# Gated sum of two state-space layers: loading the second stage's weights early, splitting SBUF between the stages, and folding C inside the first token block

## The chip, the cores and the metric

The kernel runs on one core of one Trainium2 chip, as a single launch. The metric is the device time in microseconds (us). Before the change its median over 6 runs is 695.59 us (694.76 to 696.88).

The core's engines each work through a list of instructions of their own, in order: TensorE (PE, matmul), VectorE (DVE, elementwise), ScalarE (ACT, activations and scaled copies), GpSimd (POOL) and SyncE (SP), which here only issues DMA transfers. "SPq" and "ACTq" in a profile are the queues in which SP and ACT issue them. The lists are written by a scheduler, which also decides the order within an engine; a tile pool decides when a piece of SBUF becomes free for its next user.

## The reference

One input `x` of 2048 tokens x 1024 channels goes through two layers, whose outputs are mixed by a gate per token:

```python
    x = A_x
    g = _sigmoid((x * gate_w).sum(-1, keepdims=True))
    a = _A_ref(x, A_Lambda_re, A_Lambda_im, A_B_re, A_B_im, A_C_re, A_C_im, A_log_dt, A_Dskip)
    b = _B_ref(x, B_k, B_v, B_shift_k, B_ssm_k, B_ssm_D)
    return g * a + (1 - g) * b
```

Layer A is a diagonal complex recurrence over the tokens, with a dense complex matrix before and after it:

```python
        B_bar = ((Lam_bar - 1.0) / Lam)[:, None] * Bmat
        Bu = jnp.einsum("bld,pd->blp", x + 0j, B_bar)
        ...                      # for each token t:  h = Lam_bar * h + Bu[t]
        y = 2.0 * jnp.einsum("blp,dp->bld", hseq, Cmat).real + x * Dskip[None, None, :]
```

Layer B is a short convolution of `k`, a product with `v`, a long causal convolution over all 2048 tokens (by FFT), and a product with `q`, which is `x` here:

```python
        kv = k_shift * v
        ...                      # y = irfft(rfft(kv) * rfft(ssm_k)), causal, per channel
        y = y + kv * ssm_D[None, None, :]
        return q * y
```

## The kernel before

It has two stages. Stage B does layer B in the frequency domain, in two channel halves (`dh`) of 512 channels and, in each, four time blocks of 512 tokens. The `P` operations are on DVE and the rest is matmuls with cosine and sine tables:

```python
        for dh in range(NDH):                       # NDH = 2
            ...   # kpc: 4 tiles of ssm_k by transposing DMA (two buffers); kT, vT by transposing DMA
            ...   # acc = short convolution x v (ACT tmpj, DVE acc), PE transposes it into kvT
            ...   # Kre, Kim = spectra of kpc (PE, copied out by ACT)
            for b in range(4):
                ...   # Vre, Vim = spectra of kvT (PE, copied out by ACT)
                for s in range(b, 4):
                    ...   # Pre, Pim += K x V (complex): 6 DVE operations for b = 0, else 8
                s = b
                xblkB = bxb.tile([128, NBT, DHW], BF16, name="xblkB")
                nc.sync.dma_start(out=xblkB, in_=xf[s * B:(s + 1) * B, d0:d0 + DHW]...)
                pbB = bblk.tile([128, NBT, DHW], BF16, name="pbB")
                for tl in range(NBT):               # NBT = 4
                    ...   # psc = inverse transform of P (8 or 16 matmuls)
                    cv = bblk.tile([128, DHW], BF16, name="cv")
                    nc.scalar.activation(out=cv, in_=psc, func=ACT.Copy)
                    nc.vector.tensor_tensor(out=pbB[:, tl, :], in0=cv, in1=xblkB[:, tl, :], op=ALU.mult)
                nc.sync.dma_start(out=pB_scr[...], in_=pbB)      # parked in HBM for stage A
```

Stage A opens its own pools when those of stage B have closed. It first loads and prepares weights:

```python
        nc.scalar.dma_start(out=gwb, ...)           # gate weights
        nc.scalar.dma_start(out=dsk, ...)           # Dskip
        ...   # BTre, BTim: 16 transposing DMAs of 128 x 1024, on SP
        xT_next = load_xT_block(0)                  # 8 transposing DMAs of 128 x 512, on SP
        for pi in range(NP):                        # NP = 8: rotation tables TBs, TBc
            ...   # DVE: ht, rqtab, frtab   ACT: fatab (Abs), TBs (Sin), TBc (Sin)
        for pi in range(NP):                        # folding C with the input scale
            nc.sync.dma_start_transpose(out=cre, in_=A_C_re[:, pi * 128:(pi + 1) * 128])
            nc.sync.dma_start_transpose(out=cim, in_=A_C_im[:, pi * 128:(pi + 1) * 128])
            nc.scalar.activation(out=t1, in_=cre, func=ACT.Identity, scale=col(c2r, pi))
            ...   # t2, t3, t4 alike: 4 ACT operations of 128 x 1024
            nc.vector.tensor_tensor(out=cre, in0=t1, in1=t2, op=ALU.add)
            nc.vector.tensor_tensor(out=cim, in0=t3, in1=t4, op=ALU.add)
```

Then it goes over four blocks (`tb`) of 512 tokens:

```python
            for pi in range(NP):
                ...   # bu_re, bu_im: 8 matmuls each (PE); bure, buim: copies (ACT)
                ...   # DVE: rotate (6 operations), two scans Wre and Wim, rotate back into hb_re, hb_im (6)
            for tl in range(TT_B):                  # TT_B = 4 tiles of 128 tokens
                ...   # pbb: load of pB_scr
                for dh in range(NDH):
                    ...   # psy: 16 matmuls with CrT, CiT; ACT: ga = g*psy, m_t = g*Dskip, pbs = (1-g)*pbb
                    nc.vector.tensor_tensor(out=u_t, in0=x_tt[:, d0:d0 + DHW], in1=m_t, op=ALU.mult)
                    nc.vector.tensor_tensor(out=u_t, in0=u_t, in1=ga, op=ALU.add)
                    nc.vector.tensor_tensor(out=ot[:, d0:d0 + DHW], in0=u_t, in1=pbs, op=ALU.add)
                nc.sync.dma_start(out=of[...], in_=ot)
```

Of the kernel before, what the change touches and what calls it, by code (L numbers as in the profile page):

```python
# [9 lines left out]
ALU = mybir.AluOpType  # L10
ACT = mybir.ActivationFunctionType
BF16 = mybir.dt.bfloat16
F32 = mybir.dt.float32
# [8 lines left out]
def kernel(  # L22
# [20 lines left out]
    dbg = {}  # L43
    nc = tc.nc
    xf = A_x.flatten_outer_dims()
# [3 lines left out]
    S, D = xf.shape  # L49
    P = A_Lambda_re.shape[0]  # L50
# [3 lines left out]
    ND = D // 128  # L54
    NP = P // 128
    DHW = min(512, D)
    NDH = D // DHW
    DT_H = DHW // 128
    B = S // 4
    NBT = B // 128  # L60
    NF = NBT
    NN = 2 * B - 1
    TB = min(TB_MAX, S)
# [8 lines left out]
    def col(ap, j):  # L72
        return ap[:, j:j + 1]

# [77 lines left out]
    c2r = small("c2r")  # L152
# [16 lines left out]
    with tc.tile_pool(name="tabB", bufs=1) as tabB, \  # L169
         tc.tile_pool(name="bK", bufs=1) as bK_pool, \  # L170
         tc.tile_pool(name="bKin", bufs=2) as bKin, \
         tc.tile_pool(name="bV", bufs=2) as bV_pool, \
         tc.tile_pool(name="bP", bufs=1) as bP_pool, \
         tc.tile_pool(name="bkv", bufs=2) as bkv, \
         tc.tile_pool(name="bkv1", bufs=1) as bkv1, \
         tc.tile_pool(name="bkvT", bufs=1) as bkvT_pool, \
         tc.tile_pool(name="btmp", bufs=2) as btmp, \
         tc.tile_pool(name="bblk", bufs=2) as bblk, \
         tc.tile_pool(name="bxb", bufs=2) as bxb, \
# [47 lines left out]
        for dh in range(NDH):  # L227
            d0 = dh * DHW
            kpcs = []
            for a in range(4):  # L230
                kpc = bKin.tile([128, NBT, DHW], BF16, name="kpc")
                for tl in range(NBT):
                    t0 = a * B + tl * 128
                    nc.sync.dma_start_transpose(out=kpc[:, tl, :], in_=B_ssm_k[d0:d0 + DHW, t0:t0 + 128])
                    if a == 0 and tl == 0:
                        load_kv(dh * DT_H + 1)
                if a == 0:
                    sdrow = btmp.tile([1, DHW], BF16, name="sdrow")
                    nc.scalar.dma_start(out=sdrow, in_=B_ssm_D[d0:d0 + DHW].rearrange("(o d) -> o d", o=1))
                    nc.vector.tensor_tensor(out=kpc[0:1, 0, :], in0=kpc[0:1, 0, :], in1=sdrow, op=ALU.add)  # L240
                kpcs.append(kpc)

# [49 lines left out]
            for b in range(4):  # L292
# [17 lines left out]
                for s in range(b, 4):  # L310
                    a = s - b
                    for fi in range(NF):
# [17 lines left out]
                        else:  # L330
# [14 lines left out]
                xblkB = bxb.tile([128, NBT, DHW], BF16, name="xblkB")  # L345
                nc.sync.dma_start(out=xblkB, in_=xf[s * B:(s + 1) * B, d0:d0 + DHW]
                                  .rearrange("(a p) d -> p a d", p=128))
                pbB = bblk.tile([128, NBT, DHW], BF16, name="pbB")
                for tl in range(NBT):
                    psc = bpsum.tile([128, DHW], F32, name="psc")  # L350
                    nmm = 2 * NF * (2 if s > 0 else 1)
                    cnt = 0
                    for fi in range(NF):
                        for (tab, comp) in ((CI, Pre), (SI, Pim)):
                            nc.tensor.matmul(psc, lhsT=tab[fi][:, tl * 128:(tl + 1) * 128], rhs=comp[s][fi],  # L355
                                             start=(cnt == 0), stop=(cnt == nmm - 1))
                            cnt += 1
                            if s > 0:
                                nc.tensor.matmul(psc, lhsT=tab[fi][:, B + tl * 128:B + (tl + 1) * 128],  # L359
                                                 rhs=comp[s - 1][fi], start=(cnt == 0), stop=(cnt == nmm - 1))  # L360
                                cnt += 1
                    assert cnt == nmm
                    cv = bblk.tile([128, DHW], BF16, name="cv")
                    nc.scalar.activation(out=cv, in_=psc, func=ACT.Copy)  # L364
                    nc.vector.tensor_tensor(out=pbB[:, tl, :], in0=cv, in1=xblkB[:, tl, :], op=ALU.mult)
                    if "dbg_conv" in dbg:
                        tg = s * NBT + tl
                        nc.sync.dma_start(out=dbg["dbg_conv"][tg * 128:(tg + 1) * 128, d0:d0 + DHW], in_=cv)
                nc.sync.dma_start(out=pB_scr[s * B:(s + 1) * B, d0:d0 + DHW].rearrange("(a p) d -> p a d", p=128),
                                  in_=pbB)  # L370
                if "dbg_pb" in dbg:
                    nc.sync.dma_start(out=dbg["dbg_pb"][s * B:(s + 1) * B, d0:d0 + DHW]
                                      .rearrange("(a p) d -> p a d", p=128), in_=pbB)

    with tc.tile_pool(name="aBT", bufs=1) as aBT, \
         tc.tile_pool(name="aC", bufs=1) as aC, \
         tc.tile_pool(name="tabS5", bufs=1) as tabS5, \
         tc.tile_pool(name="axt", bufs=2) as axt, \
         tc.tile_pool(name="axl", bufs=2 * TT_B) as axl, \
         tc.tile_pool(name="ahb", bufs=2) as ahb, \  # L380
         tc.tile_pool(name="abu", bufs=3) as abu, \
         tc.tile_pool(name="awk", bufs=2) as awk, \
         tc.tile_pool(name="atiny", bufs=4) as atiny, \
         tc.tile_pool(name="cblk", bufs=3) as cblk, \
         tc.tile_pool(name="apsum", bufs=2, space=bass.MemoryType.PSUM) as apsum:
# [6 lines left out]
        nc.scalar.dma_start(out=gwb, in_=gate_w.rearrange("(j p) -> p j", p=128))  # L392
        dsk = aC.tile([128, D], BF16, name="dsk")
        nc.scalar.dma_start(out=dsk, in_=A_Dskip.partition_broadcast(128))

        BTre, BTim = [], []
        for dt_ in range(ND):
            bre = aBT.tile([128, P], BF16, name=f"BTre{dt_}")
            nc.sync.dma_start_transpose(out=bre, in_=A_B_re[:, dt_ * 128:(dt_ + 1) * 128])
            BTre.append(bre)  # L400
        for dt_ in range(ND):
            bim = aBT.tile([128, P], BF16, name=f"BTim{dt_}")
            nc.sync.dma_start_transpose(out=bim, in_=A_B_im[:, dt_ * 128:(dt_ + 1) * 128])
            BTim.append(bim)
# [11 lines left out]
        with tc.tile_pool(name="tabtmp", bufs=2) as tabtmp:  # L416
            for pi in range(NP):
# [4 lines left out]
                fr = tabtmp.tile([128, TB], F32, name="frtab")  # L422
                nc.vector.tensor_tensor(out=fr, in0=ht, in1=rq, op=ALU.subtract)
# [10 lines left out]
        with tc.tile_pool(name="cwk", bufs=2) as cwk:  # L434
            for pi in range(NP):
                cre = aC.tile([128, D], BF16, name=f"CrT{pi}")
                nc.sync.dma_start_transpose(out=cre, in_=A_C_re[:, pi * 128:(pi + 1) * 128])
                cim = aC.tile([128, D], BF16, name=f"CiT{pi}")
                nc.sync.dma_start_transpose(out=cim, in_=A_C_im[:, pi * 128:(pi + 1) * 128])
                t1 = cwk.tile([128, D], BF16, name="c_t1")  # L440
                t2 = cwk.tile([128, D], BF16, name="c_t2")
                nc.scalar.activation(out=t1, in_=cre, func=ACT.Identity, scale=col(c2r, pi))
                nc.scalar.activation(out=t2, in_=cim, func=ACT.Identity, scale=col(mc2i, pi))
                t3 = cwk.tile([128, D], BF16, name="c_t3")
                t4 = cwk.tile([128, D], BF16, name="c_t4")
                nc.scalar.activation(out=t3, in_=cim, func=ACT.Identity, scale=col(mc2r, pi))
                nc.scalar.activation(out=t4, in_=cre, func=ACT.Identity, scale=col(mc2i, pi))  # L447
                nc.vector.tensor_tensor(out=cre, in0=t1, in1=t2, op=ALU.add)  # L448
                nc.vector.tensor_tensor(out=cim, in0=t3, in1=t4, op=ALU.add)
                CTr.append(cre)  # L450
                CTi.append(cim)

        for tb in range(NTB):
# [4 lines left out]
            for tl in range(TT_B):  # L458
                tt_ = tt0 + tl
                x_tt = axl.tile([128, D], BF16, name="x_tt")  # L460
                (nc.sync if tt_ % 2 == 0 else nc.scalar).dma_start(out=x_tt, in_=xf[tt_ * 128:(tt_ + 1) * 128, :])
                x_tiles.append(x_tt)
# [12 lines left out]
            for pi in range(NP):  # L475
# [59 lines left out]
                nc.vector.tensor_tensor(out=hb_im[:, pi, :], in0=u3, in1=u4, op=ALU.add)  # L535
                if "dbg_h" in dbg:
                    nc.sync.dma_start(out=dbg["dbg_h"][pi * 128:(pi + 1) * 128, c0:c0 + TB], in_=hb_re[:, pi, :])
            for tl in range(TT_B):
# [3 lines left out]
                (nc.scalar if tt_ % 2 == 0 else nc.sync).dma_start(out=pbb, in_=pB_scr[tt_ * 128:(tt_ + 1) * 128, :])  # L542
                ot = cblk.tile([128, D], BF16, name="ot")
                for dh in range(NDH):
# [18 lines left out]
                    nc.vector.tensor_tensor(out=u_t, in0=x_tt[:, d0:d0 + DHW], in1=m_t, op=ALU.mult)  # L563
                    nc.vector.tensor_tensor(out=u_t, in0=u_t, in1=ga, op=ALU.add)
                    nc.vector.tensor_tensor(out=ot[:, d0:d0 + DHW], in0=u_t, in1=pbs, op=ALU.add)  # L565
# [37 lines left out]
```

## Time and profile before

| | |
|---|---|
| median of 6 runs | 695.59 us |
| span of the profiled run | 694.1 us |
| PE busy | 500.3 us (72%) |
| DVE busy | 551.1 us (79%) |
| ACT busy | 323.4 us (47%) |
| SP queue (q1) | 41.96 MB, 26.2% of the 16 DMA engines' span |
| mean granted TensorE clock | 0.901 |

Busy time is a sum over a span with several regimes, so the table alone doesn't say what a change in one of them is worth. The same numbers are therefore also to be had by stretch of time, and there is a chain of work: followed back from the last instruction, at each step to what released it, or to the instruction before it on its engine. Lines such as "L448" are lines of the kernel; "x8" is how often. An operation's mean time and the distance from one start to the next differ a little, since neighbours overlap.

### The profile page before, as it was taken

What the parts mean: (1) busy time and instruction counts of PE and PEld (TensorE: products, weight loads), DVE (VectorE), ACT (ScalarE), POOL (GpSimd) and SP (SyncE); (2) the same over time, 40 slices, a digit from 0 to 9 for tenths busy, and PEclk for the clock granted to TensorE, in tenths of its full rate; (3) what the DMA queues carried; (4) which work ended last, traced back from release to release, by engine and by line L of the source; (5) the groups of instructions that cost most, each with busy time, mean ns of one, the idle gap of its engine ahead of it and who ended that gap; (6) DMA issues with size and microseconds to landing.
All of it is one profiled execution on the core that took longest, in us unless ns stands there. A gap on an engine that the chain in (4) does not pass through costs nothing.

```text
span 694.1 us, 6996 instructions
## 1 busy us (share of the span) xinstructions
PE 500.3 (72%) x2240; PEld 213.5 (31%) x2240; DVE 551.1 (79%) x1464; ACT 323.4 (47%) x487; POOL 1.7 (0%) x8
## 2 busy tenths in 40 slices
PE   0223989786877998867650349699959996999477
PEld 0011434332333443322220014244424442444123
DVE  4896309999995279999951229999999999999962
ACT  4878964404049854221056885126504540554033
POOL 0000000000000000000000000000000000000000
PEclk9999999999989899998985568989989996999879
DMA  8734341010116100201099684203220210011001
GB/s 158 152 77 92 63 108 19 9 53 30 32 61 153 31 0 1 61 0 62 30 166 216 142 162 148 61 1 107 76 61 31 92 60 0 32 61 31 1 15 45
DMA packets 122744, 46.87 MB, mean 68 GB/s; under 512 B 108242, under 2 KB 116436, under 8 KB 122708
## 3 DMA queue, kind: packets, MB, share of 16 engines
q1 hardware_dynamic: 114944, 41.96, 26.2%
q10 hardware_dynamic: 7764, 4.48, 2.7%
q8 instruction: 17, 0.28, 0.2%
q14 instruction: 19, 0.16, 0.1%
HBM read 12.86 MB, written 8.39 MB: 31 GB/s over the span
## 4 chain that ended last, share of the span: by engine, by line
DVE 63%; PE 16%; SPq 9%; ACT 6%; issue 4%; DMA 2%; ACTq 0%; DVEq 0%
DVE Wim L521 5%; DVE Wre L519 5%; PE ps_re L278 3%; PE ps_im L281 3%; DVE t L339 2%; DVE t L333 2%; DVE Pre L334 2%; DVE t L336 2%; DVE Pim L340 2%; DVE t L342 2%; DVE Pim L343 2%; DVE Pre L337 2%; PE psy L553 2%; PE psy L550 2%; ACT tmpj L258 2%
## 5 line engine op out<-in xcount | busy, mean ns | idle before, releaser
L550 PE MATMUL psy<-CrT,hb_re 128*128 128x512 bf16 x256 | 101.9, 404 | 35.2 <-DVE hb_re L530 34.7
L553 PE MATMUL psy<-CiT,hb_im 128*128 128x512 bf16 x256 | 102.6, 408 | 0.6 <-DVE hb_im L535 0.6
L481 PE MATMUL bu_re<-xT_b,BTre 128*128 128x512 bf16 x256 | 71.1, 408 | 0.1
L355 PE MATMUL psc<-Pre,TT 128*128 128x512 bf16 x128 | 50.0, 393 | 23.3 <-DVE Pre L337 21.8
L484 PE MATMUL bu_im<-xT_b,BTim 128*128 128x512 bf16 x256 | 62.7, 387 | 0.0
L364 ACT ACTIVATE cv<-psc 128x512 bf16<-128x512 f32 x32 | 17.8, 597 | 88.9 <-DVE t L336 46.2
L355 PE MATMUL psc<-Pim,TS 128*128 128x512 bf16 x128 | 49.4, 389 | 4.9 <-DVE Pim L343 4.3
L258 ACT ACTIVATE tmpj<-kT,skc 128x2047 bf16<-128x2047 bf16 (+2 forms) x24 | 46.8, 1994 | 8.6 <-DVE acc L260 5.3
L266 PE MATMUL pt<-ident,acc 128*128 128x128 bf16 x128 | 14.5, 269 | 48.9 <-DVE acc L261 42.0
L550 PEld LDWEIGHTS <-hb_re 128*128 128x128 bf16 x256 | 25.6, 102 | 72.2 <-DVE hb_re L530 42.3
L302 PE MATMUL ps_im<-kvT,TS 128*128 128x512 bf16 x128 | 36.4, 405 | 14.6 <-ACT Vim L307 14.6
L307 ACT ACTIVATE Vim<-ps_im,wsc 128x512 bf16<-128x512 f32 x32 | 22.0, 687 | 50.0 <-DVE t L339 25.2
L281 PE MATMUL ps_im<-kpc,TS 128*128 128x512 bf16 x128 | 37.5, 411 | 10.5 <-ACT TS L219 8.7
L469 PE MATMUL psg<-gwb,xT_b 128*128 128x1 bf16 x128 | 7.2, 169 | 47.0 <-DMA xT_b<-in_A_x_dram 36.8
L561 ACT ACTIVATE pbs<-pbb,omg 128x512 bf16<-128x512 bf16 x32 | 22.9, 723 | 37.9 <-DVE ot L565 30.2
L278 PE MATMUL ps_re<-kpc,TT 128*128 128x512 bf16 x128 | 37.9, 410 | 3.4 <-DMA kpc<-in_B_ssm_k_dram 2.0
L359 PE MATMUL psc<-Pre,TT 128*128 128x512 bf16 x96 | 38.4, 400 | 0.0
L359 PE MATMUL psc<-Pim,TS 128*128 128x512 bf16 x96 | 37.6, 391 | 0.0
L553 PEld LDWEIGHTS <-hb_im 128*128 128x128 bf16 x256 | 26.1, 102 | 36.6 <-issue 7.5
L299 PE MATMUL ps_re<-kvT,TT 128*128 128x512 bf16 x128 | 36.9, 412 | 0.6 <-ACT Vre L306 0.6
L488 ACT ACTIVATE bure<-bu_re 128x512 bf16<-128x512 f32 x32 | 19.1, 596 | 37.7 <-DVE r_t L500 18.3
L448 DVE TENSOR_TENSOR CrT<-c_t,c_t 128x1024 bf16<-128x1024 bf16 x8 | 5.5, 693 | 39.1 <-ACT c_t L447 39.1
(165 smaller groups left out, 1040.7 us busy)
## 6 DMA issues: line engine op xcount, KB each, us to landing
xblkB<-in_A_x_dram SPq DMA_DIRECT2D x8, 512.0 KB, 4.7
pB_scr<-pbB SPq DMA_DIRECT2D x8, 512.0 KB, 3.2
out_dram<-ot SPq DMA_DIRECT2D x16, 256.0 KB, 2.0
pbb<-pB_scr ACTq DMA_DIRECT2D x8, 256.0 KB, 2.7
x_tt<-in_A_x_dram SPq DMA_DIRECT2D x8, 256.0 KB, 3.0
x_tt<-in_A_x_dram ACTq DMA_DIRECT2D x8, 256.0 KB, 3.0
pbb<-pB_scr SPq DMA_DIRECT2D x8, 256.0 KB, 2.7
kpc<-in_B_ssm_k_dram SPq DMA_TRANSPOSE x32, 2.7
```

Source lines behind the costliest of these rows:

```text
L258: nc.scalar.activation(out=tmpj[:, j:S], in_=kT[:, 0:S - j], func=ACT.Identity, scale=col(skc, j))
L278: nc.tensor.matmul(ps_re, lhsT=CF[tl][:, fi * 128:(fi + 1) * 128], rhs=kpc[:, tl, :], start=(tl == 0), stop=(tl == NBT - 1))
L281: nc.tensor.matmul(ps_im, lhsT=SF[tl][:, fi * 128:(fi + 1) * 128], rhs=kpc[:, tl, :], start=(tl == 0), stop=(tl == NBT - 1))
L299: nc.tensor.matmul(ps_re, lhsT=CF[tl][:, fi * 128:(fi + 1) * 128], rhs=kvT[:, b * NBT + tl, :], start=(tl == 0), stop=(tl == NBT - 1))
L302: nc.tensor.matmul(ps_im, lhsT=SF[tl][:, fi * 128:(fi + 1) * 128], rhs=kvT[:, b * NBT + tl, :], start=(tl == 0), stop=(tl == NBT - 1))
L355: nc.tensor.matmul(psc, lhsT=tab[fi][:, tl * 128:(tl + 1) * 128], rhs=comp[s][fi], start=(cnt == 0), stop=(cnt == nmm - 1))
L359: nc.tensor.matmul(psc, lhsT=tab[fi][:, B + tl * 128:B + (tl + 1) * 128], rhs=comp[s - 1][fi], start=(cnt == 0), stop=(cnt == nmm - 1))
L481: nc.tensor.matmul(ps_re, lhsT=BTre[dt_][:, pi * 128:(pi + 1) * 128], rhs=xT_b[:, dt_, :], start=(dt_ == 0), stop=(dt_ == ND - 1))
L484: nc.tensor.matmul(ps_im, lhsT=BTim[dt_][:, pi * 128:(pi + 1) * 128], rhs=xT_b[:, dt_, :], start=(dt_ == 0), stop=(dt_ == ND - 1))
L519: nc.vector.tensor_tensor_scan(out=Wre, data0=rcol_bc, data1=pre_re, initial=init_re, op0=ALU.mult, op1=ALU.add)
L550: nc.tensor.matmul(psy, lhsT=hb_re[:, pi, tl * 128:(tl + 1) * 128], rhs=CTr[pi][:, d0:d0 + DHW], start=(cnt == 0), stop=(cnt == n_mm - 1))
L553: nc.tensor.matmul(psy, lhsT=hb_im[:, pi, tl * 128:(tl + 1) * 128], rhs=CTi[pi][:, d0:d0 + DHW], start=(cnt == 0), stop=(cnt == n_mm - 1))
```

## The change

It has five parts.

1. The transposed input matrices `BTre` and `BTim` get a pool that is open for the whole kernel, and their 16 loads are written in stage B, before the second channel half's work.
2. The pools of both stages are put on two sides of SBUF. What stage B is done with first (`kpc`, `kT`, `vT`, `acc`, `kvT`) lies on the right, and the first things that stage A needs (rotation tables, `xT_b`, `bure`, work tiles) take that side over. The rest of stage A goes to the left, where stage B's tables and spectra were. To make room, the rotation tables reuse a buffer (`fr = rq`), and the fold of C works in place with one buffer.
3. The fold of C is no longer a loop of its own: `fold_C(pi)` is called in the first token block, after the scan work of the same `pi`.
4. Stage B no longer multiplies by `x`. It parks the convolution itself, and stage A multiplies the sum of both terms by `x` once: `ot = x*(g*Dskip + (1-g)*conv) + g*psy`. The load `xblkB` and the product `pbB` fall away; the number of DVE operations in stage A stays at three.
5. All DMA transfers of stage A are issued by SP; ACT issues none there.

The diff, cut to its core:

```diff
+    aBT = ctx.enter_context(tc.tile_pool(name="aBT", bufs=1))
+    BTre = [aBT.tile([128, P], BF16, name=f"BTre{i}") for i in range(ND)]
+    BTim = [aBT.tile([128, P], BF16, name=f"BTim{i}") for i in range(ND)]
+    def emit_BT_loads():
+        for dt_ in range(ND):
+            nc.sync.dma_start_transpose(out=BTre[dt_], in_=A_B_re[:, dt_ * 128:(dt_ + 1) * 128])
+        ...                                       # BTim alike
     # stage B's pools: tabB, bP, bblk, bV, btmp, bK on the left
+         tc.tile_pool(name="bKin", bufs=2, side="right") as bKin, \
+         ...                                       # bkv, bkv1, bkvT: side="right"; bxb is gone
+            if dh == NDH - 1:
+                emit_BT_loads()
-                xblkB = bxb.tile([128, NBT, DHW], BF16, name="xblkB")
-                nc.sync.dma_start(out=xblkB, ...)
-                    cv = bblk.tile([128, DHW], BF16, name="cv")
-                    nc.scalar.activation(out=cv, in_=psc, func=ACT.Copy)
-                    nc.vector.tensor_tensor(out=pbB[:, tl, :], in0=cv, in1=xblkB[:, tl, :], op=ALU.mult)
+                    nc.scalar.activation(out=cvB[:, tl, :], in_=psc, func=ACT.Copy)
                 nc.sync.dma_start(out=pB_scr[...],
-                                  in_=pbB)
+                                  in_=cvB)
     # stage A's pools
+    with tc.tile_pool(name="tabS5", bufs=1, side="right") as tabS5, \
+         ...                                       # axt, abu, awk, atiny: side="right"
+         tc.tile_pool(name="cwk", bufs=1) as cwk, \
-        nc.scalar.dma_start(out=gwb, ...)
+        nc.sync.dma_start(out=gwb, ...)            # dsk, x_tt and pbb alike
-                fr = tabtmp.tile([128, TB], F32, name="frtab")
-                nc.vector.tensor_tensor(out=fr, in0=ht, in1=rq, op=ALU.subtract)
+                nc.vector.tensor_tensor(out=rq, in0=ht, in1=rq, op=ALU.subtract)
+                fr = rq
-            for pi in range(NP):
-                cre = aC.tile([128, D], BF16, name=f"CrT{pi}")
-                ...                                # two loads, four ACT operations, two DVE adds
+        def fold_C(pi):
+            ...                                    # the same two loads
+            nc.scalar.activation(out=t1, in_=cre, func=ACT.Identity, scale=col(c2r, pi))
+            nc.scalar.activation(out=t4, in_=cre, func=ACT.Identity, scale=col(mc2i, pi))
+            nc.scalar.activation(out=cre, in_=cim, func=ACT.Identity, scale=col(mc2i, pi))
+            nc.scalar.activation(out=cim, in_=cim, func=ACT.Identity, scale=col(mc2r, pi))
+            nc.vector.tensor_tensor(out=cre, in0=cre, in1=t1, op=ALU.add)
+            nc.vector.tensor_tensor(out=cim, in0=cim, in1=t4, op=ALU.add)
                 nc.vector.tensor_tensor(out=hb_im[:, pi, :], in0=u3, in1=u4, op=ALU.add)
+                if tb == 0:
+                    fold_C(pi)
-                    nc.vector.tensor_tensor(out=u_t, in0=x_tt[:, d0:d0 + DHW], in1=m_t, op=ALU.mult)
-                    nc.vector.tensor_tensor(out=u_t, in0=u_t, in1=ga, op=ALU.add)
-                    nc.vector.tensor_tensor(out=ot[:, d0:d0 + DHW], in0=u_t, in1=pbs, op=ALU.add)
+                    nc.vector.tensor_tensor(out=u_t, in0=m_t, in1=pbs, op=ALU.add)
+                    nc.vector.tensor_tensor(out=u_t, in0=u_t, in1=x_tt[:, d0:d0 + DHW], op=ALU.mult)
+                    nc.vector.tensor_tensor(out=ot[:, d0:d0 + DHW], in0=u_t, in1=ga, op=ALU.add)
```

## The prediction

> **What bounds the kernel now.** I first read the shares of the chain of work that ended last, then cut the span where the chain changes its kind and asked for each engine's busy time in those stretches. The page says of the chain:
>
> ```profile
> DVE 63%; PE 16%; SPq 9%; ACT 6%; issue 4%; DMA 2%; ACTq 0%; DVEq 0%
> ```
>
> Mostly DVE, but a good tenth is a DMA queue (SPq, DMA), with which no matrix work goes on. The stretches (start:end, length, then busy us of PE, PE's weight loads, DVE, ACT, POOL with counts, granted clock, DMA share, GB/s) show where:
>
> ```profile
> 0.00:102.50 102.50, 44.40 (x200) 20.04 (x201) 57.93 (x122) 75.88 (x90) 1.71 (x8) 1.00 0.54 108
> 102.50:203.50 101.00, 80.97 (x343) 33.53 (x342) 100.50 (x300) 31.46 (x52) 0.00 (x0) 0.93 0.14 37
> 203.50:247.00 43.50, 39.41 (x205) 18.55 (x203) 18.62 (x22) 37.74 (x52) 0.00 (x0) 0.92 0.33 74
> 247.00:348.40 101.40, 77.83 (x309) 31.20 (x308) 100.92 (x300) 27.19 (x43) 0.00 (x0) 0.92 0.08 26
> 348.40:417.00 68.60, 21.08 (x84) 7.76 (x84) 19.53 (x35) 50.12 (x63) 0.00 (x0) 0.63 0.92 176
> 417.00:666.00 249.00, 213.19 (x1005) 92.42 (x1004) 244.38 (x666) 88.82 (x172) 0.00 (x0) 0.91 0.17 52
> 666.00:694.10 28.10, 23.45 (x99) 9.99 (x99) 9.27 (x22) 12.20 (x18) 0.00 (x0) 0.93 0.10 37
> ```
>
> The seven are: a head (loads, short convolution, spectra of K); the products of the first half; a middle like the head; the products of the second half; a gap; stage A; a tail. DVE fills the products (100.5 of 101.0, 100.92 of 101.4) and stage A. In the gap it works 19.53 of 68.60 us, and the DMA engines are full (0.92). The chain in order of time (start, length) names the gap's cause:
>
> ```profile
> 348.11 1.17 SPq L437
> 349.33 2.39 SPq L439
> ...
> 386.47 1.26 SPq L409
> ...
> 398.24 4.96 DMA CiT<-in_A_C_im_dram
> ...
> 413.78 1.04 ACT c_t L447
> 415.00 1.28 ACT L471
> ```
>
> SP issues 10 loads of C, 16 of B and 8 of xT one by one at some 1.3 us (348 to 396.9); then come the last C load, the folding on ACT, and the gate's table load. Only then do DVE's rotations start. The costs I need are in the groups by line (busy us, mean ns | idle before):
>
> ```profile
> L365 DVE TENSOR_TENSOR pbB<-cv,xblkB 128x512 bf16<-128x512 bf16 x32 | 13.2, 418 | 10.4 <-ACT cv L364 10.3
> L448 DVE TENSOR_TENSOR CrT<-c_t,c_t 128x1024 bf16<-128x1024 bf16 x8 | 5.5, 693 | 39.1 <-ACT c_t L447 39.1
> L425 ACT ACTIVATE fatab<-frtab 128x512 f32<-128x512 f32 x8 | 4.9, 613 | 0.0
> ```
>
> In the time order of DVE, neighbours of 416 ns start every 0.336 us (101.0/300 in the second stretch), and the two adds of a fold 0.61 us apart; on ACT the four scaled copies start every 1.04 us.
>
> **What the Trainium skill says.** "DMA: Bandwidth & Descriptors", section "Issuing engines are not separate DMA queues": transfers started by different engines run on the same 16 DMA engines, and issuing from several saves only sequencer time. So part 5 gains or loses issue time at most; the gap's DMA share of 0.92 agrees that the engines, not the issuers, were full. "VectorE: DVE Perf Modes", "The perf-mode tier table": a bf16 tensor_tensor of 2048 takes 1224 ns in its best mode; the trace has 1220 ns at L261, so no DVE operation here becomes cheaper by being moved. "ScalarE: Activation LUTs", "What ACT_TABLE_LOAD costs": 1283 ns each; the trace has 1283. Both kernels have three. "Perfetto Trace Analysis", "Optimization Strategy", advises interleaving regimes whose bound differs. That is this change: a DMA-full gap goes under DVE-bound stretches that use 0.08 to 0.17 of the DMA.
>
> **The change, part by part.** I call E the moment of DVE's last product of stage B (348.4 before). What lies where I took from the instruction order of the built kernel, durations from the trace.
>
> *Head.* SP's order now has BT loads after the eight kpc loads: one, kT of job 2, one, its vT, then twelve in a row before kT of job 3. kpc ends at 19.95 before. From there: 1.34 + 2.9 + 1.34 + 3.3 + 12 x 1.34 = 25.0, so that kT is issued at about 45 instead of 32.8 and lands 4.6 us later, at 49.6. ACT first needed it at 48.7. The delay is about 1 us. Against it, 4.2 us of early table work on DVE (four ht, four rqtab, two frtab) leaves the head; it can't help while the load is late. Head: +1.
>
> *Products.* Twelve of the pbB products lie in each of the two full DVE stretches, four more in the middle and four in the gap. 2 x 12 x 0.336 = 8.1 us saved. The eight others are beside other work.
>
> *Middle.* PE's order has one more pair of spectra of the second half inside the first half's last inverse transform; they come at 0.86 us each: -1.7. Together E moves to 348.4 + 1 - 8.1 - 1.7 = 339.6.
>
> *Gap.* xT of blocks 0 and 1 (16 loads, 20.8 us of issue) stands in SP's order after the store of the second block of the second half (315.5 before), so it lands about at E; B has long been there. What is left is ACT: two cv copies, eight tables, two cv, the table load, the gate, bure. DVE's first table input is ready at E + 2.2 (ht x2, rqtab x2, one subtraction); a table triple takes 1.65 us on ACT (distance between L425 starts); so 2.2 + 8 x 1.65 + 2 x 0.5 = 16.4, + 1.3 table load, + 0.7 gate and bure = E + 18.4. PE has its last inverse transform done by E + 8.5 and the first bu by E + 12.5, inside this. Before, the rotations started at 417.05 = E + 68.65. Saved: 50.2.
>
> *Fold.* Its 16 adds now stand in DVE's list in the first block: 8 x 2 x 0.61 = +9.8. ACT needs 4 x 1.04 + 2 x 0.5 per pi, 5.2 us, and DVE 6.4 + 1.2 = 7.6 us, so ACT keeps up; a pair of C loads takes 2.6 us of SP per pi, so they do too.
>
> *Stage A and tail.* The rest of stage A stays 249 us: three DVE operations per half tile as before. In the tail only one of them follows ga, not two: -0.4. I add 2 us for waits that the new interleaving makes.
>
> Sum: 1 - 8.1 - 1.7 - 50.2 + 9.8 - 0.4 + 2 = -47.6, so 695.6 - 47.6 = 648.0 us.
>
> **Rivals.** *The early loads hold up the head.* For it: SP is one ordered queue, twelve transposes stand before a load that ACT waits for, and DMA share was already 0.9 in the first 20 us. If they go at 2 us rather than 1.34, kT is 8 us later and the time 656. Against it: in the gap the same loads went at 1.34 with the engines full.
>
> *The fold makes the first block ACT- or load-bound.* ACT's list puts the fold's copies between bure and buim of later pi, and fold 5 to 7 behind gate results of blocks 1 and 2, which wait for PE and for xT of block 2. If each of eight pi lost 2 us, the time would be 664. Against it: ACT has 2.4 us to spare per pi, xT of block 2 can be issued as soon as block 0's last bu is done, some 25 us before the gate needs it.
>
> *One queue for all transfers.* pbb and x_tt now stand behind output stores that wait for DVE. If they came late, DVE would wait in stage A, which it hardly does now (of its 18.7 us for ga, 17 are in the tail). Three pbb and eight x_tt buffers speak against it; I'd give it 0 to 8 us.
>
> *Less gain in the gap.* If xT landed late or the tables waited for space, the rotations might start at E + 30 rather than 18: 660. The other way, tables fully under the last transform would give E + 12: 642.
>
> **Range and chances.** The gap's 50 us is the largest term and stands on loads that are simply elsewhere; the losses I can name cost up to 16 us each and are not likely together. So 640 to 660, with 648 in it. Two per cent faster is 681.7, which would need over two thirds of the gain to be lost: faster 0.96, same 0.03, slower 0.01.
>
> **What would show it.** Right: products stretches of about 97 us; a gap of 18 to 20 us between DVE's last Pim and first rotation, with ACT's Sin tables in it and no BT load; a first block of about 61 us rather than 52; a tail of 28. Wrong in the head: ACT tmpj waiting for kT by more than 2 us. Wrong in the fold: DVE idle before its CrT adds, for ACT. Wrong in the queue: waits of PE or ACT for xT_b, pbb or x_tt. If the gap still shows loads on the chain, the split of SBUF did not free space in time, and the whole sum falls.

## The result, and the profile after

The changed kernel takes 642.38 us (median of 8 runs, 639.64 to 643.60) against 695.75 us (median of 16 runs) for the kernel before: a ratio of 0.9229, 95% interval 0.9214 to 0.9243. Predicted were 648.0 us, in a range of 640 to 660. The profiled run spans 642.0 us, that of before 694.1.

The chain that ended last, by engine, in the changed kernel:

```profile
DVE 68%; PE 15%; ACT 7%; SPq 4%; issue 4%; DMA 2%; ACTq 0%; DVEq 0%
```

SPq has gone from 9 to 4%. The seven stretches, cut at the same events as before (start:end, length, then busy us of PE, PE's weight loads, DVE, ACT, POOL, granted clock, DMA share, GB/s):

```profile
0.00:102.84 102.84, 45.38 (x201) 19.89 (x202) 54.88 (x112) 74.64 (x88) 1.71 (x8) 1.00 0.75 139
102.84:199.65 96.81, 79.68 (x341) 33.22 (x340) 96.37 (x288) 32.97 (x53) 0.00 (x0) 0.95 0.09 22
199.65:243.25 43.60, 39.27 (x207) 18.44 (x206) 17.24 (x19) 36.65 (x51) 0.00 (x0) 0.96 0.32 61
243.25:340.50 97.25, 78.21 (x309) 31.44 (x308) 96.78 (x288) 27.65 (x43) 0.00 (x0) 0.91 0.16 38
340.50:359.00 18.50, 15.72 (x85) 7.11 (x84) 12.01 (x25) 17.39 (x34) 0.00 (x0) 1.00 0.67 145
359.00:612.06 253.06, 211.15 (x1005) 92.27 (x1004) 252.64 (x681) 118.15 (x201) 0.00 (x0) 0.93 0.25 64
612.06:642.00 29.94, 25.14 (x100) 10.41 (x99) 9.66 (x24) 12.94 (x20) 0.00 (x0) 0.84 0.09 35
```

Read down the lengths: head 102.8 (102.5 before), products 96.8 (101), middle 43.6 (43.5), products 97.3 (101.4), gap 18.5 (68.6), stage A 253.1 (249), tail 29.9 (28.1). The gap gives 50 us of the 52. In it ACT is now busy 17.39 of 18.50 us. The chain in order of time (start, length) says with what:

```profile
340.16 0.43 DVE Pim L354
...
353.05 0.61 ACT TBc L426
353.67 0.52 ACT fatab L422
...
356.97 1.28 ACT L466
358.50 0.49 ACT bure L483
```

Table triples one behind the other, the gate's table load, then the first `bure`; no load of B, C or xT is left on the chain between DVE's last product (its end is E, 340.5 here) and its first rotation at 359.02. The 16 loads of xT were issued from 306.44 to 328.1, 12 us before E; the prediction had them land about at E. The fold's adds are in stage A: 16 adds, on average 0.602 us from start to next start, together 9.6 us.

| step of the sum (us) | predicted | measured |
|---|---|---|
| head | +1 | +0.3 |
| products | -8.1 | -8.2 |
| middle | -1.7 | 0.0 |
| gap | -50.2 | -50.2 |
| fold | +9.8 | +9.6 |
| rest of stage A | +2 | -5.5 |
| tail | -0.4 | +1.8 |
| sum | -47.6 | -52.1 |

The measured column is the difference of the two profiled runs, taken at the events themselves; the cuts of the stretches above are rounded, so their lengths differ from it by up to 0.2 us. "Rest of stage A" is what remains of its lengths, 253.0 - 248.9 = +4.1, after the fold's 9.6. The total came out 5.6 us under the predicted one, and "rest of stage A" is the largest part of that.

### The profile page after: what moved, and what is told of

The parts are those of the page before. It is cut to its first block, busy times and chain, and to the rows that moved or that the text cites. A ratio compares the mean times of both kernels' runs of the same rounds, so it can differ in the third digit from the quotient of the medians.

```text
span 642.0 us, 6914 instructions
## 1 busy us (share of the span) xinstructions
PE 494.6 (77%) x2240; PEld 212.8 (33%) x2240; DVE 539.6 (84%) x1432; ACT 320.4 (50%) x487; POOL 1.7 (0%) x8
## 4 chain that ended last, share of the span: by engine, by line
DVE 68%; PE 15%; ACT 7%; SPq 4%; issue 4%; DMA 2%; ACTq 0%; DVEq 0%
DVE Wim L516 6%; DVE Wre L514 5%; PE ps_re L289 3%; PE ps_im L292 3%; DVE t L344 2%; DVE Pre L345 2%; DVE t L350 2%; DVE t L347 2%; DVE Pre L348 2%; DVE Pim L354 2%; DVE Pim L351 2%; DVE t L353 2%; PE psy L547 2%; PE psy L550 2%; DVE t L334 2%
## 5 line engine op out<-in xcount | busy, mean ns | idle before, releaser
L547 PE MATMUL psy<-CrT,hb_re 128*128 128x512 bf16 x256 | 101.1, 401 | 38.3 <-DVE hb_re L525 33.6
L550 PE MATMUL psy<-CiT,hb_im 128*128 128x512 bf16 x256 | 100.8, 401 | 0.0
L476 PE MATMUL bu_re<-xT_b,BTre 128*128 128x512 bf16 x256 | 65.4, 391 | 2.4 <-ACT bure L483 2.4
L479 PE MATMUL bu_im<-xT_b,BTim 128*128 128x512 bf16 x256 | 64.7, 393 | 1.9 <-ACT buim L484 1.9
L371 ACT ACTIVATE cvB<-psc 128x512 bf16<-128x512 f32 x32 | 18.2, 595 | 93.8 <-PE psc L367 82.7
L363 PE MATMUL psc<-Pre,TT 128*128 128x512 bf16 x128 | 50.2, 395 | 15.6 <-DVE Pre L348 14.2
L363 PE MATMUL psc<-Pim,TS 128*128 128x512 bf16 x128 | 49.8, 392 | 4.9 <-DVE Pim L354 4.3
L556 ACT ACTIVATE m_t<-dsk,gcols 128x512 bf16<-128x512 bf16 x32 | 23.0, 718 | 53.0 <-DVE u_t L560 53.0
L289 PE MATMUL ps_re<-kpc,TT 128*128 128x512 bf16 x128 | 39.3, 420 | 1.9 <-DMA kpc<-in_B_ssm_k_dram 1.2
L271 DVE TENSOR_TENSOR acc<-acc,tmpj 128x2047 bf16<-128x2047 bf16 (+2 forms) x24 | 29.3, 1223 | 11.8 <-ACT tmpj L269 11.0
L367 PE MATMUL psc<-Pre,TT 128*128 128x512 bf16 x96 | 38.3, 399 | 0.0
L479 PEld LDWEIGHTS <-BTim 128*128 128x128 bf16 x256 | 25.7, 101 | 34.3 <-issue 6.8
```

What stands on the lines that cost most here:

```text
L289: nc.tensor.matmul(ps_re, lhsT=CF[tl][:, fi * 128:(fi + 1) * 128], rhs=kpc[:, tl, :], start=(tl == 0), stop=(tl == NBT - 1))
L476: nc.tensor.matmul(ps_re, lhsT=BTre[dt_][:, pi * 128:(pi + 1) * 128], rhs=xT_b[:, dt_, :], start=(dt_ == 0), stop=(dt_ == ND - 1))
L479: nc.tensor.matmul(ps_im, lhsT=BTim[dt_][:, pi * 128:(pi + 1) * 128], rhs=xT_b[:, dt_, :], start=(dt_ == 0), stop=(dt_ == ND - 1))
L547: nc.tensor.matmul(psy, lhsT=hb_re[:, pi, tl * 128:(tl + 1) * 128], rhs=CTr[pi][:, d0:d0 + DHW], start=(cnt == 0), stop=(cnt == n_mm - 1))
L550: nc.tensor.matmul(psy, lhsT=hb_im[:, pi, tl * 128:(tl + 1) * 128], rhs=CTi[pi][:, d0:d0 + DHW], start=(cnt == 0), stop=(cnt == n_mm - 1))
```

## Experiments: what holds the gap

**B shares space with stage B again** (its pool opens with stage A, on the left):

```diff
-    aBT = ctx.enter_context(tc.tile_pool(name="aBT", bufs=1))   # open for the whole kernel
-            if dh == NDH - 1:
-                emit_BT_loads()
+         tc.tile_pool(name="aBT", bufs=1) as aBT, \              # with stage A's pools, left
+        emit_BT_loads()                                          # after the load of dsk
```

> The changed kernel, but with the B matrices back in a pool that is opened with stage A, on the left, where they take over the space of stage B's tables; all else as changed. Theory (what counts is that B is there before stage B ends): their 16 loads can't start before PE's last inverse transform, some 8.5 us after DVE's last product E, and go one by one at 1.34 us; the last lands at about E + 33, so the first rotation is at E + 35 instead of E + 18.5 and the time is about 642.4 + 16.5 = 659 us (655 to 664). Rival 1 (freed space and early xT are enough, B's loads would hide too): at most 646. Rival 2 (B costs its full issue time of 16 x 1.34 = 21 us and more, because C's loads mix in): 664 or more. If the early loads hold up the head, it gets shorter here by the 0.3 us that it grew.

Measured: 657.88 us, ratio 0.9454 (0.9436 to 0.9472); E is at 339.82. Its chain shows the loads of B one by one, after DVE's last product, and the landing of the last:

```profile
369.93 1.33 SPq L397
371.31 3.87 DMA BTim<-in_A_B_im_dram
377.71 1.14 DVE Wre L512
```

The first rotation, which needs `BTre` alone, is at E + 26.4, but the first scan, which needs both, is at E + 37.8; in the changed kernel it is at E + 20.5. By the medians (657.88 - 642.38) the place that B has of its own is worth 15.5 us, as the theory had it. The head without these loads takes 102.76 us, with them 102.84: a cost to it is not to be seen. The edit also moves the place in the program where the loads are written, but that doesn't matter: with `emit_BT_loads` written at stage A's start, but B in its own space, the scheduler puts the 16 loads at the very same places in SP's list (read from the built kernel, not run).

**All pools on one side:**

```diff
-         tc.tile_pool(name="bKin", bufs=2, side="right") as bKin, \
+         tc.tile_pool(name="bKin", bufs=2) as bKin, \
         ...                            # and for every other pool with side="right"
```

> The changed kernel with all pools on one side of SBUF again, B still loaded early and for the whole kernel. Theory: the rotation tables and xT now wait for space that PE's last inverse transform holds (E + 8.5), and the eight table triples follow it, 8 x 1.65, then 1.3 for the table load and 0.7: first rotation at about E + 24, time about 648 us (645 to 653). Rival 1 (the split is what hides the loads): xT comes behind C loads as in the kernel before, the gap grows by 20 us or more, 662 or more. Rival 2 (the split does nothing once B is early): 642.

Measured: 653.45 us, ratio 0.9393 (0.9368 to 0.9417), just above the range. The gap is 27.4 us, not 24, and DVE then waits 3.5 us for the first `buim`. The chain names the load of C first and the load of xT last:

```profile
340.91 6.14 DMA CrT<-in_A_C_re_dram
...
361.48 0.53 SPq L398
362.05 3.23 DMA xT_b<-in_A_x_dram
365.76 0.43 PE bu_im L479
```

I had expected the tables to end last. They are late, but the last wait is xT, as rival 1 said, at half of its size: without the split, xT comes behind six loads of C.

**The fold as a loop ahead of the blocks:**

```diff
+        for pi in range(NP):
+            fold_C(pi)
         for tb in range(NTB):
...
-                if tb == 0:
-                    fold_C(pi)
```

> The changed kernel with the fold of C as a loop of its own ahead of the token blocks, as before the change, with the changed kernel's in-place arithmetic. Theory: B and xT are already there, so C's loads hold up nothing; ACT mixes the fold's copies of 1.04 us with the gate and bure: first bure some 3 us later, its buim some 12 us later, but fewer of the adds (0.6 us each) stand in the first block, some 6 of 16 move into the gap: +9 us, about 651 (646 to 656). Rival 1 (the fold as a loop puts all of its 33 us of ACT ahead of the rotations): 665 or more. Rival 2 (the scheduler makes the same of both): 642.

Measured: 650.08 us, ratio 0.9336 (0.9317 to 0.9354), as expected: the gap is 21.8 us, the first scan comes at E + 33.1, and in stage A DVE idles 6.2 us, nearly all of it before adds of the fold, for ACT.

**The third part alone, on the kernel before:**

```diff
+                if tb == 0:
+                    fold_C(pi)                 # in-place arithmetic and the rq buffer as in the change
```

> The kernel before, with the third part of the change alone (fold of C inside the first token block, with the in-place fold and the rq buffer to make room). Theory (one part alone brings little, since the loads of B and xT still stand in the gap and only six of C's sixteen can go behind them): 34 loads of 1.33 us, the last xT at about E + 48, first rotation at about E + 52 instead of E + 68.7, and the fold's adds +9.65 in the first block: about 689 us (684 to 693). Rival (the fold and C's loads were the gap's cause): C's 16 loads and the ACT work behind them all go, 35 us or more less: 670 or less.

Measured: 685.13 us, ratio 0.9844 (0.9823 to 0.9864). The gap falls from 68.7 to 51.2 us, and the chain in it still ends with a load, the last one of xT:

```profile
393.32 3.62 DMA xT_b<-in_A_x_dram
398.16 2.99 PE bu_im L482 x7
```

Together: undone one at a time, the three parts cost 15.5, 11.1 and 7.7 us by the medians, 34 in all; the third alone brings 10.8. The gap's 50 us aren't a sum of parts. The loads stand in one queue, and the gap is short only when none that the first rotations need (B, xT) is left in it. The first loads of C are issued inside the gap in the changed kernel too, from 350.24, and hold up nothing there.

## Experiments: the products, the queue and the fold

**The fourth part undone**, with the old order of the last three operations and with `ga` last:

```diff
+                    nc.vector.tensor_tensor(out=cvB[:, tl, :], in0=cvB[:, tl, :], in1=xblkB[:, tl, :], op=ALU.mult)
...
+                    nc.vector.tensor_tensor(out=u_t, in0=x_tt[:, d0:d0 + DHW], in1=m_t, op=ALU.mult)
+                    # old order: + ga, then + pbs       second kernel: + pbs, then + ga
```

> The changed kernel with the fourth part undone: stage B multiplies by x again (load xblkB, one DVE product per 128 x 512 tile) and stage A ends with the old order x*m_t, + ga, + pbs. Theory: 24 products of 0.336 us come back into the two full DVE stretches, 8.1 us; and stage A gets back the 4 to 5 us in which DVE waited for ga or for a neighbour's result, less some 2 us of the tail: about 653 to 654 us (651 to 657). Rival 1 (the shorter stage A had nothing to do with the order of the last three operations): 650.5. Rival 2 (the products were beside other work): 643.

> As the kernel with the fourth part undone, but with ga added last (x*m_t, + pbs, + ga). The number of DVE operations is the same in both. Theory (order of the last three operations lets DVE do two of them without waiting for ga): 8.1 us more than the changed kernel, about 650.5 us (649 to 652.5), that is 2 to 4 us faster than the one with the old order, and no DVE wait for ga between the first rotation and the tail. Rival (order does nothing): the same as the other within 1 us.

Measured: 652.29 us, ratio 0.9360 (0.9343 to 0.9377), and 650.91 us, ratio 0.9344 (0.9326 to 0.9361). The products are worth what was predicted: each full DVE stretch is longer by 4.0 us, and both kernels are 8.5 to 10 us slower than the changed one. But stage A takes 252.76 and 252.90 us, and 253.03 in the changed kernel. The order of the last three operations did not shorten it: after seeing the result I had thought so, and that theory falls. The two intervals overlap.

**The fifth part undone:**

```diff
-        nc.sync.dma_start(out=dsk, ...)
+        nc.scalar.dma_start(out=dsk, ...)             # gwb, half of x_tt and of pbb alike
```

> The changed kernel with the fifth part undone: gwb, dsk, and half of the x_tt and pbb loads are issued by ACT again. Theory: nobody waits for these loads in the changed kernel, so 642 us, within 1.5 us. Rival 1 (ACT's issues cost it time in the gap, where it is the bound: gwb and dsk): 643 to 645. Rival 2 (one queue delays pbb behind stores): 635 to 640.

Measured: 644.77 us, ratio 0.9260 (0.9231 to 0.9289), an interval that overlaps with that of the changed kernel. In its profile the gap is 21.7 instead of 18.5 us: between the last `TBc` and the gate's table load ACT issues two loads of `x_tt` and computes nothing for 2.95 us. The issues themselves take 0.37 and 0.33 us. Before each, ACT waits for the landing of an earlier transfer of SP, of `pB_scr` at 354.54 and of `CiT` at 356.46, as the chain shows for the second (L456 is the issue, L466 the table load):

```profile
352.57 3.89 DMA CiT<-in_A_C_im_dram
356.48 0.33 ACTq L456
356.84 1.28 ACT L466
```

ACT doesn't use the data of either; by the trace each issue waits for the semaphore by which the earlier transfer tells of its landing, and raises the same one itself. That is rival 1, in a place other than I named (`x_tt`, not `gwb` and `dsk`). The total does not prove that it costs time; the profile makes it likely.

**The fold's adds on GpSimd:**

```diff
-            nc.vector.tensor_tensor(out=cre, in0=cre, in1=t1, op=ALU.add)
-            nc.vector.tensor_tensor(out=cim, in0=cim, in1=t4, op=ALU.add)
+            nc.gpsimd.tensor_tensor(out=cre, in0=cre, in1=t1, op=ALU.add)
+            nc.gpsimd.tensor_tensor(out=cim, in0=cim, in1=t4, op=ALU.add)
```

> The changed kernel with the 16 adds of the fold on GpSimd, which is idle, instead of DVE. Theory (the fold is on the path only by its 16 DVE adds of 0.6 us): the first block loses 9.65 us: about 633 us (631 to 636), 8 pi steps of about 6.4 us instead of 7.58. Rival 1 (GpSimd is so slow that ACT, which waits for the one buffer c_t, or PE at the block's end is held up): 640 or more. Rival 2 (work on GpSimd slows DVE's operations by as much): 642.

Measured: 670.89 us, ratio 0.9630 (0.9609 to 0.9652), 28 us slower than the changed kernel. DVE in order of time, beside the first pair of adds (which run on GpSimd from 361.16 for 2.35 us and from 363.47 for 2.31):

```profile
361.51 2.28 DVE L528 TENSOR_TENSOR r_t<-TBs,Wre 128x512 bf16<-128x512 bf16 x1
...
363.78 2.28 DVE L524 TENSOR_TENSOR r_t<-TBs,Wim 128x512 bf16<-128x512 bf16 x1
```

The same operations take 0.41 us otherwise; each add on GpSimd holds one of them for 2.28. Two per pi are 3.74 us, and the first block's steps are 10.12 us, which is 6.38 + 3.74. Against the changed kernel's 7.58 that is 20 us in eight steps. Another 8 us are idle time of DVE where blocks 1 to 3 begin, of a kind that comes up again below. The Trainium skill has this in "SBUF — State Buffer", section "SBUF: two separate sides": the two share a port pair as an exclusive lock, taken for a whole instruction also by a DVE operation with two SBUF inputs against a GpSimd one that reads SBUF. The trace agrees; rival 2 was right in kind and too small.

**The fold's adds on PE**, by diagonal matrices, summed in PSUM:

```diff
+            nc.tensor.matmul(pfr, lhsT=dg[0], rhs=cre[:, h0:h0 + 512], start=True, stop=False)
+            nc.tensor.matmul(pfr, lhsT=dg[1], rhs=cim[:, h0:h0 + 512], start=False, stop=True)
             ...                                        # pfi alike; both from the psy buffers
+            nc.scalar.activation(out=cre[:, h0:h0 + 512], in_=pfr, func=ACT.Copy)
```

> The changed kernel with the fold's adds on PE: C's two loaded matrices are multiplied by diagonal matrices and summed in PSUM (8 matmuls of 0.22 us per pi), and ACT copies four results of 0.6 us instead of four scaled copies of 1.04; no fold work on DVE, and none on GpSimd. Theory (the fold is on the path only by its 16 DVE adds, and the run with GpSimd failed because DVE stood still beside it): first block's steps 6.4 us instead of 7.58, about 633.5 us (631.5 to 637). Rival 1 (PE, 53 of 61 us busy in the first block, becomes its bound with 13.8 us more): 640 to 645. Rival 2 (the adds hid other waits, which now show): 638 to 642.

Measured: 650.81 us, ratio 0.9347 (0.9329 to 0.9364), 8.4 us slower. The steps of the first block are 6.38 us, as expected, so the fold does cost its adds there. But the step from the last pi of this block to the first of the next takes 32.4 us instead of 12.1. These are the block's steps and the stretch behind them (columns as in the stretches above):

```profile
357.30:412.10 54.80, 47.91 (x237) 20.21 (x235) 50.90 (x128) 33.86 (x82) 0.00 (x0) 0.92 0.56 120
412.10:440.00 27.90, 27.89 (x143) 12.85 (x144) 15.40 (x55) 20.03 (x35) 0.00 (x0) 1.00 0.40 125
```

PE isn't full in the first and DVE is half idle in the second. In PE's time order all 128 psy matmuls of block 0 stand ahead of block 1's first `bu` (435 us); in the changed kernel some `bu` come first (415 to 420), and DVE works on them while PE does psy. So neither rival is right as written: what was gained was lost to the order of PE's list.

## Experiments: gap and tail of the changed kernel

**Tables inside the first block, its gate behind it:**

```diff
+            if tb > 0:
+                gates()                               # block 0: after its pi loop
...
             for pi in range(NP):
+                if tb == 0:
+                    make_table(pi)
```

> The changed kernel with the rotation tables made inside the first block's pi loop, and the gate of the first block written after that loop. Theory (the gap is ACT's chain of eight table triples and the gate's table load, 1.65 us each and 1.28): the first rotation then waits for five triples and PE's first bu (E + 12.5), so it starts at about E + 13.5 to 14.5 instead of E + 18.5, and the remaining triples run beside DVE's block: -4 us, about 638 us (636.5 to 640.5). Rival (the triples that are left then hold up bure of later pi, or the gates the end of the block): 642 or more.

Measured: 640.57 us, ratio 0.9199 (0.9177 to 0.9222), an interval that overlaps with that of the changed kernel. The first scan comes at E + 15.5 instead of E + 20.5, so the gap's 5 us are there. They were given back later: the next section says where.

**Three psy buffers:**

```diff
-                    psy = apsum.tile([128, DHW], F32, name="psy")
+                    psy = apsum.tile([128, DHW], F32, name="psy", bufs=3)
```

> The changed kernel with three instead of two PSUM buffers for psy. Theory (the tail grew by 1.8 us because PE stopped for 0.7 us, waiting for ACT to empty psy behind m_t and pbs, and then ran another 5 us at half speed): no stop, PE at full speed some 3 us earlier, tail 27.5 to 28.5 instead of 29.95, -2 us, about 640.4 (639.5 to 641.5). Rival (the slow stretch comes from the idle time before it and the stop adds only itself): -0.7 us, 641.7.

Measured: 637.45 us, ratio 0.9160 (0.9143 to 0.9178), faster than both kernels. The tail is 25.4 instead of 29.9 us. PE in the changed kernel, around the end of the last block (start, us; 612.05 is DVE's last `hb_im`):

```profile
611.77 0.61 PE L547 MATMUL psy<-CrT,hb_re 128*128 128x512 bf16 x1 [5.86 <-DVE hb_re L525]
...
614.37 0.58 PE L547 MATMUL psy<-CrT,hb_re 128*128 128x512 bf16 x1 [0.72 <-ACT ga L554]
...
619.84 0.38 PE L550 MATMUL psy<-CiT,hb_im 128*128 128x512 bf16 x1
```

Only two half tiles could be summed up to the last pi before the end; then PE stopped for 0.72 us, until ACT had emptied a buffer, behind `m_t` and `pbs`. It ran at 0.43 us a matmul to 619.4, then at 0.22. With three buffers there is no stop (0.7 us), and a third half tile is summed ahead up to the last pi, so that 86 instead of 100 matmuls are left: 14 x 0.216 = 3.0 us less after the end. Of these 86, 14 run at half speed instead of 17, another 0.6. My expectation had the stop and forgot the third half tile.

**Tables, fold on PE and three buffers together** (the three edits above in one kernel):

> Tables inside the first block, fold on PE and three psy buffers together. Theory (gap, first block and tail are three different stretches, so the gains add): 642.4 - 4 - 9 - 2 = 627.5 us (625 to 632). Rival (in the first block, tables, fold and bu copies all want ACT, so that part is lost): 632 to 638.

Measured: 648.66 us, ratio 0.9324 (0.9301 to 0.9347). The step behind the first block is 38.3 us: the loss of the fold on PE is in it, and the gains in gap (5 us) and tail (5.3) don't make it up. The best version is the changed kernel with three psy buffers.

## Why the prediction was right, and which terms were off

**Right, with number:** the gap (first rotation at E + 18.5, predicted E + 18.4), the fold, the products. Reading ACT's list in the gap and counting triples gave the end of a 68 us stretch to 0.1 us, because ACT alone was the bound once the loads were elsewhere. It was no luck of terms that cancel: the first table input was ready at E + 2.2, the triples ended at E + 16.5, and the table load, the gate and `bure` took the 2.05 us after it, all as predicted. The experiments above show that the loads of B or of xT would have taken ACT's place.

**Head, +1:** kT was issued at 44.37, as predicted (about 45), landed at 49.2 and was in time for ACT, which came to it at 49.8; the wait for kT that the prediction named did not come. ACT waited elsewhere. Its waits in the first 104 us, in the changed kernel and then in the kernel before (total, times, longest):

```profile
ACT kvT L278 <- DMA BTim<-in_A_B_im_dram: 5.2, 1, 5.2
ACT tmpj L269 <- DMA kpc<-in_B_ssm_k_dram: 5.1, 1, 5.1
```

```profile
ACT tmpj L258 <- DVE acc L260: 5.3, 3, 2.4
...
ACT tmpj L258 <- DVE acc L261: 3.3, 1, 3.3
```

The copy `kvT` doesn't read BTim or wait for kT. In ACT's list the issue of a small load (`skb`) stands before it, and the trace has ACT's sequencer, which steps through this list, waiting there from 35.8 to 42.6, when a load of BTim landed, for a semaphore that both loads raise: the same kind of wait as in the kernel with two queues. So loads in SP's queue can hold up ACT by way of ACT's own transfers, a path that the prediction didn't have. In return, of ACT's 8.6 us of waits for DVE's `acc` all but 1.7 went, and the head came out 0.3 longer. Heads of kernels with the same loads vary from 100.8 to 102.8 us between profiles, so 0.3 is not resolved.

**Middle, -1.7:** this step failed. I took the one more pair of K spectra to be moved into time that PE had free. In both kernels PE is full there: its last inverse transform of the half took 20.2 us (191.06 to 211.28) with the pair in it, 18.0 (194.87 to 212.82) without. The 1.7 us were paid earlier instead of later.

**Rest of stage A, +2:** this term is mis-sized; it measured -5.5. The prediction took stage A of the kernel before as full, with 17 of DVE's 18.7 us of waits for `ga` in the tail. That was misread: 15.5 are in the tail and 3.2 before it (417 to 665.9 us, then from 666):

```profile
DVE u_t L564 <- ACT ga L557: 3.2, 3, 1.5
...
DVE u_t L564 <- ACT ga L557: 15.5, 7, 3.0
```

In the kernel before, DVE idled 3.8 us where blocks 2 and 3 begin, of 4.2 us in all of stage A. The chain shows how: ACT's `pbs` waits for the buffer that DVE's `ot` frees, and `m_t` and `ga` stand behind it in ACT's list.

```profile
556.65 0.43 DVE ot L565
557.11 0.72 ACT pbs L561
557.83 0.61 ACT m_t L559
558.44 0.58 ACT ga L557
559.05 0.44 DVE u_t L564
```

One half tile costs ACT 1.9 us in this way, and DVE 1.4 us for its last three operations. In DVE's list of the kernel before these operations come 6 and then 11 or 12 between the first scans of blocks 2 and 3, and none later, so DVE runs into ACT; in the changed kernel they come 6, 7 and 1, and 0.4 us of idle time is left in the whole of stage A. In such a bunch, each that uses a result just made also starts 0.46 instead of 0.34 us after it, about 1 us more. Another 0.7 us are only moved: two of these operations stand behind DVE's last `hb_im` now (24 in the tail, 22 before). Together that is 5.5 us.

The kernel with tables in the first block shows the converse: it has the bunch again (6, 11 and 6, 12), DVE idles 1.57, 1.57 and 0.87 us in the same places, and that is where most of its 5 us went (from the first scan on, stage A is 6.4 us longer, the tail 2.9 us shorter). The kernel with the adds on GpSimd has it in three blocks, and idles there. The kernel before with the third part alone has 6, 6 and 4, and no such idle time. So bunch and idle time go together in all these runs, but no run changes this order alone. The orders of blocks 2 and 3 were there to be read in the built kernel; I read those of gap and first block, and added 2 us for the rest. Why the scheduler bunches in some kernels and not in others is open: it does it with the fold inside the block and without, and it spreads in kernels with either order of the last three operations and either number of queues.

**Tail, -0.4:** also mis-sized, it measured +1.8. The step counted DVE's operations behind `ga`, but the tail goes by PE: both kernels have 100 matmuls left, of which 17 instead of 10 run at half speed (7 x 0.21 = 1.5 us), and PE stops for 0.72 instead of 0.19 us. With three psy buffers the stop was gone and the tail 25.4 us.

**One queue, 0 to 8 us:** the rival did not come true; in the gap and stage A of the changed kernel no wait is put down to a DMA. But what the prediction said of part 5, "issue time at most", is too little: with two queues ACT lost 2.95 us in the gap, of which 0.7 are issues.

## What to carry to other kernels

When a stage boundary is full of loads, give the next stage's first operands space that is free before the boundary, all of them: here the loads of B or of xT, left behind alone, took the place of the rest. With loads gone, the next bound is the engine's list across the boundary, which can be counted from its order. Read that order for every block, not for the first alone, and after every edit: here 5 to 20 us came and went with the order of DVE's or PE's list. And look where an engine that computes also issues transfers: its issue can wait for a transfer of another queue.

## What the hardware did that I had not expected

- One 128 x 1024 add on GpSimd (2.3 us) held a 128 x 512 DVE operation of 0.41 us for 2.28 us; DVE scans (1.2 us) beside such adds kept their length, and there it was the add that grew, to 3.1 to 5.4 us.
- ACT's issue of a load waited for the landing of an earlier transfer of SP that ACT had no use for: until 42.6 us in the head of the changed kernel, and twice in the gap with two queues (354.54 and 356.46).
- PE at half speed (0.43 us a matmul) in the tail lasted 4.7 us from its start at 665.21 in the kernel before, and 8.1 us from 611.77 in the changed one, where a stop of 0.72 us lies in between. The Trainium skill ("TensorE: Matmul & The Clock Gate", section "What's actually happening") gives about 3.4 us of sustained work in a free-running window; these stretches are longer. With three psy buffers, without the stop, it lasted 5.9 us (609.42 to 615.29). That the stop restarts the wait fits, but was not tested by itself.
